# Gradient of a gated block with a long convolution, one core: dh for two slabs per matmul, dw stored by ScalarE's queue

## The chip, the core and the metric

The kernel runs as one program on one core of a Trainium2 chip. The metric is the device time of an execution in microseconds (us); every kernel is run several times. Nothing but this kernel runs on the core during a measurement.

The core's engines are named as the profile names them: PE (TensorE, matmuls), PEld (the weight loads of those matmuls), DVE (VectorE), ACT (ScalarE), POOL (GpSimd) and SP (SyncE). Each runs its own instructions in order. SP, ACT and POOL also issue transfers (DMAs); the profile writes "SPq", "ACTq" and "POOLq" for that.

## The reference

What is computed is the forward result of one block and its gradients for nine inputs. The block takes x of 2048 rows and 1024 columns, and weights of 1024 by 3584 (gate, up) and 3584 by 1024 (down):

```python
x = A_q
xn = _layernorm(x, axis=-1)
s = _A_ref(xn, A_k, A_v, A_shift_k, A_ssm_k, A_ssm_D)   # shift by 4 taps, long convolution, times xn
g = _silu(_B_ref(xn, B_w_gate, B_w_up, B_w_down))
return x + s * g

def _B_ref(x, w_gate, w_up, w_down):
    g = jnp.einsum("bsd,df->bsf", x, w_gate)
    u = jnp.einsum("bsd,df->bsf", x, w_up)
    h = g * u
    return jnp.einsum("bsf,fd->bsd", h, w_down)
```

and the outputs are `_out` with the nine results of `jax.vjp(_f, ...)(grad_out)`. The part that matters here is the gradient of the gated product: dh = dbm @ w_down transposed (dbm is the gradient of the block's B result), then dg = dh * u and du = dh * g, then the weight gradients dw_gate = xn transposed @ dg, dw_up = xn transposed @ du, and dw_down = h transposed @ dbm.

## The kernel before

The hidden width of 3584 is cut into 14 slabs (`NSL`) of 256 columns (`SLW`). The kernel runs in stages that overlap:

1. 0 to about 515 us: layer norm, the gate and up products slab by slab (`gu_unit`, L671), and beside them on DVE the forward convolution (`conv_forward`). The products g and u of each slab go to DRAM (`GUd`), as do h and its transpose.
2. To about 700 us: the down product (`bm_mm`, L1034) and, row block by row block, the gate's derivative on DVE (`gate`). dbm goes to DRAM and comes back transposed (`DBMT`, four tiles of 512 rows).
3. 700 to about 1317 us, the stage of the change: `dh_half` (L1471 to L1493) and `dw_slab` (L1495 to L1512).
4. To about 1498 us: dw_down (`dwd_mm`, L1582). Then dx (`dx_part`, L1644) with the layer norm's backward, to the end at 1909.9 us. Beside it DVE computes the gradients of the shift (`dk_units`).

Stage 3 in detail. For a slab and one half of the rows (1024), `dh_half` makes dh in two groups `g` of four row blocks. One PSUM tile `psb` (128 by 512 values) holds two row blocks `x` of 256 columns: 16 matmuls of 256 columns (L1482), whose moving operand is `wdt`, w_down of this slab transposed by the load (`load_wdt`, L1330). ACT copies the tile to `dht` (L1484). `multiply` then multiplies, on DVE, g and u of that half slab (`dgu`, loaded from `GUd` by `gu_in`) by dh, in place, for four row blocks at a time; after the second group the product is stored to `DGd`, from which stage 4 loads it again.

`dw_slab` makes dw_gate and dw_up of a slab together: for each of eight `dc` it adds 16 matmuls of 512 columns (L1499: 256 of gate, 256 of up) over the 16 row blocks. The first 8 read the first half slab, the last 8 the second half. ACT copies the tile to `wb` (L1504), and after each second `dc` two transfers of 128 KB on SP's queue store it (L1508).

The two are interleaved: after each `dc` group, `next(others, None)` lets the generator of the next slab's dh run one group `g`, so that the four dh groups of the next slab lie behind `dc` 0 to 3, and `dc` 4 to 7 follow with no dh between them. `todo` holds the multiplies; `after_group` puts them on DVE after the next group of matmuls, and then calls `btick`, which advances `conv_backward` on DVE by as much as `BT` says (2 ticks for a dw group, 1 for a dh tile). From L1530 on, DVE's instructions keep this program order (`PIN`). `conv_backward` (L1103) begins with the eight transforms of `dy_forward`, each of which ends with a store `DYFd<-DX` on POOL's queue (L1101), and goes on with 16 units of `product` (whose first tile is `m`, L342) and `inv8`.

The loads of `GUd` for later half slabs are issued on SP after each `dw_slab` (L1546), one `wdt` load after `dc` 3 (L1511). The five tiles U11, U6, U2, U3 and U12 take the half slabs in turn.

`Wbc` (L128, loaded at L152) holds the four taps of the shift for all 1024 channels on every partition. `shift` (L762) and `dk_units` (L1230) read it.

SP's, POOL's and ACT's transfers use a common set of eight completion semaphores per kind (hardware queues of SP and ACT; POOL's own), taken in turn: a transfer waits, on its issuing engine, until the earlier one of the same semaphore has landed.

Of the kernel before, what the change touches and what calls it, by code (L numbers as in the profile page):

```python
# [19 lines left out]
def build_kernel(  # L20
# [11 lines left out]
    nc = tc.nc  # L32
# [92 lines left out]
    nc.scalar.activation(warm[:], warm[:], ACT.Sqrt)  # L125
    RSTD = const.tile([P, NB], F32, name="RSTD")
    RSTN = const.tile([P, NB], F32, name="RSTN")
    Wbc = const.tile([P, 4, D], BF16, name="Wbc")  # L128

    tip = tc.alloc_tile_pool(name="tip", bufs=1)  # L130
    TI = tip.tile([P, 2, 8, 2, P], BF16, name="TI")
# [9 lines left out]
    def load_bcast(bsb):  # L141

        wrow = bsb.tile([1, D, 4], BF16, name="wrow")
        st(wrow[:].rearrange("p d j -> p (d j)"), A_shift_k.rearrange("(o d) j -> o (d j)", o=1))
        wtap = bsb.tile([1, 4, D], BF16, name="wtap")

        def turn(j):
            nc.gpsimd.tensor_copy(wtap[:, j, :], wrow[:, :, j])

        def spread():  # L150
            st(WTd.rearrange("(o x) -> o x", o=1), wtap[:].rearrange("p j d -> p (j d)"))
            st(Wbc[:].rearrange("p j d -> p (j d)"), bass.AP(WTd.tensor, WTd.offset, [[0, P], [1, 4 * D]]))  # L152
        return turn, spread

    def angles(tg):
# [378 lines left out]
    Dz = kst.tile([P, D], BF16, name="Dz")  # L534
    V.memset(Dz[:], 0.0)
    krow = kst.tile([P, 2, 11, 256], BF16, name="k")
    V.memset(krow[0:1, 0, 0:3, :], 0.0)
    bsb = pool("bc_sb", 1)
    tg = pool("tg", 1)
# [200 lines left out]
    def conv_forward():  # L740
        S_ = conv_state

        def load_kv(dp, c):
            S_["k", dp] = krow
            if dp > 0 or c == 0:
                for i in range(2) if dp == 0 else (c,):
                    cld_k(krow[:, i], i, dp)
            if dp > 0 or c == 1:
                for i in range(2) if dp == 0 else (c,):
                    v = U[4][:, 2048 * i:2048 * i + 2048].rearrange("p (a x) -> p a x", a=8)  # L750
                    cld_v(v, i, dp * 256, 256)
# [6 lines left out]
        def shift(dp):  # L758
            kv = cx.tile([P, NB, 256], BF16, name="kv")
            S_["kvt", dp] = kv  # L760
            k = S_.pop(("k", dp))
            wb = lambda j: Wbc[:, j:j + 1, dp * 256:(dp + 1) * 256].unsqueeze(1).to_broadcast([P, 2, 8, 256])  # L762
# [12 lines left out]
            yield 2.3  # L775
# [294 lines left out]
    while conv_state["filters"]:  # L1070
        bm_first([fc_])
        fc_ += 1
    bw = pool("bw", 2, side="right")
    mh = [pool("mh0", 1, side="right")]
    ps_bx = pool("ps_bx", 1, space=PSUM)

# [106 lines left out]

    def dh_tail(ds, G, ew):
        hr = ew.tile([P, 2, 8, P], BF16, name="yl")
        ho = ew.tile([P, 2, P, 8], BF16, name="ho")
# [12 lines left out]
        st(o_dssmk[ds * P:(ds + 1) * P, :], ho[:].rearrange("p c u r -> p (c u r)"))  # L1199
        yield 0.0  # L1200
# [3 lines left out]
    def dk_units(ew):  # L1204
# [9 lines left out]
        def load_turned(i):  # L1214
# [7 lines left out]
                nc.sync.dma_start_transpose(out=dkT[:], in_=DKSHd[ds, c * H:c * H + H, :])  # L1222
            return kT, dkT

        dk = load_rows(0)
        yield 3
        for i in range(16):
            ds, c = divmod(i, 2)
            dsl = slice(ds * P, (ds + 1) * P)
            wb = lambda j: Wbc[:, j:j + 1, dsl].to_broadcast([P, 8, P])  # L1230
# [95 lines left out]
            defer(turn)  # L1326

    def load_wdt(sl):
        wdt = bw.tile([P, DC, SLW], BF16, name="wdt")
        wdt_ld[0] = nc.sync.dma_start_transpose(out=wdt[:], in_=B_w_down[sl * SLW:(sl + 1) * SLW, :])  # L1330
        return wdt

    def load_ht(bp):
        ht = mh[bp % 2].tile([P, NF, 256], BF16, name="ht")
# [1 line left out]
            last = ld(ht[:, f0:f1], ht_rows(bp, f0, f1))  # L1336
        return (lambda fc: ht[:, fc]), last

    DGU = {}
    wdts = []  # L1340
    wdt_ld = [None]

    def gu_in(k):

        if k < 2 * NSL:
            t = U[(11, 6, 2, 3, 12)[k % 5]][:].rearrange("p (a b f) -> p a b f", b=8, a=2)
            ld(t, GUd[k // 2, k % 2])
            DGU[k] = t

    with tc.issue_after(ht1[1].ins):  # L1350
        ht2 = load_ht(2)
    bm_first(range(fc_, NF))
    room = [bw.tile([P, DC, SLW], BF16, name="wdt")[:].rearrange("p (i x) f -> p i (x f)", i=2) for i in range(2)]
# [61 lines left out]
    for bp in range(2, 8):  # L1415
# [6 lines left out]
        with tc.issue_after(row_ld[0].ins):  # L1422
            if bp in (4, 5, 7):
                q = (4, 5, 7).index(bp)
                dma_t = nc.sync.dma_start_transpose(out=DBMT[q], in_=DBMd[512 * q:512 * q + 512, :])
            if bp == 6:
                wdts.append(load_wdt(0))
                dma_t = wdt_ld[0]
        with tc.issue_after(dma_t.ins) if dma_t is not None else nullcontext():
            rows_in[2 * bp + 1] = gate_rows(2 * bp + 1)  # L1430
        if bp > 5:
            with tc.issue_after(row_ld[0].ins):
                gu_in(0) if bp == 6 else wdts.append(load_wdt(1))
        for i in range(2):
            n = (2 * bp + i - 2) * NF
            while done < n + NF:
# [11 lines left out]

    XN = [u8(q, a=4) for q in (7, 0, 1, 9)]
    bg = pool("bg", 2, side="right")  # L1450
    U.append(bg.tile([P, 4096], BF16, name="U12", bufs=1))
    ps_b = ps_tr = pool("ps_b", 4, space=PSUM)
    tr_name[0] = "psb"
    ps_c3 = pool("ps_c3", 2, space=PSUM)
# [6 lines left out]
        bpump((bcnt[0] - 10) / (BT - 10))  # L1461

    todo = []

    def after_group(n):
        flush(2)
# [1 line left out]
            todo.pop(0)()  # L1468
        btick(n)

    def dh_half(k, wdt):  # L1471

        sl, hf = divmod(k, 2)
        dgu = DGU[k]
        for g in range(2):
            dht = bg.tile([P, 4, SLW], BF16, name="dht", bufs=3)
            for e in range(2):
                ps = ps_b.tile([P, 512], F32, name="psb")
                for x in range(2):
                    b = 4 * g + 2 * e + x  # L1480
                    for dc in range(DC):
                        nc.tensor.matmul(ps[:, x * SLW:(x + 1) * SLW], DBMT[2 * hf + g][:, dc, (b % 4) * P:(b % 4 + 1) * P],  # L1482
                                         wdt[:, dc, :], start=(dc == 0), stop=(dc == DC - 1))
                nc.scalar.copy(out=dht[:, 2 * e:2 * e + 2].rearrange("p b f -> p (b f)"), in_=ps[:])  # L1484
                after_group(1)

            def multiply(g=g, dht=dht):
                bs = slice(4 * g, 4 * g + 4)
                tt(dgu[:, :, bs], dgu[:, :, bs], dht[:].unsqueeze(1).to_broadcast([P, 2, 4, SLW]), MUL)
                if g == 1:  # L1490
                    ld(DGd[sl, :, 1024 * hf:1024 * hf + 1024, :].rearrange("a (u b) f -> u a b f", u=P), dgu)
            todo.append(multiply)
            yield  # L1493

    def dw_slab(sl, dgus, others):  # L1495
        for dc in range(DC):
# [21 lines left out]

    for e in later:
        e[0] = -2  # L1520
    for k in (1, 2):
        gu_in(k)
    for q in range(4):
        ld(XN[q], xnn[:, q // 2, 4 * (q % 2):4 * (q % 2) + 4, :])
    for k in (3, 4):
        gu_in(k)
    DBM = [u8(q, a=4) for q in (10, 8, 4, 5)]
    HSL = (3, 11, 6)
    hs = {}
    PIN[0] = PINQ[0] = True  # L1530
    for k in range(2):
        run(dh_half(k, wdts[0]))
    todo.pop()()
    for sl in range(NSL):
        if sl + 1 == NSL:
            load_h(0)
            for q in range(4):
                ld(DBM[q], DBMd[512 * q:512 * q + 512, :].rearrange("(b u) d -> u b d", u=P))
            load_h(1)

        def halves():
            for k in (2 * sl + 2, 2 * sl + 3):
                if k < 2 * NSL:
                    yield from dh_half(k, wdts[sl + 1])
        dw_slab(sl, [DGU[2 * sl], DGU[2 * sl + 1]], halves())
        for k in (2 * sl + 5, 2 * sl + 6):  # L1546
            gu_in(k)
# [260 lines left out]
```

## Time and profile before

| | |
|---|---|
| runs | 1911.66 us median of 3 (1911.64 to 1913.55) |
| the profiled execution | 1911.63 us, of which 1909.9 us are the span of its instructions |
| granted clock of TensorE | 1.0 of full speed |
| PE, DVE, ACT, POOL busy | 1899.4, 1549.7, 636.8, 332.7 us |
| bytes moved | 444.34 MB, mean 233 GB/s |
| stage 3 | 700 to 1317 us |

How to read it: the span is the time from the first to the last instruction that the profile shows; what lies around it is 1911.63 - 1909.9 = 1.7 us. A group line gives the source line, the engine, the operation, output and input tiles, shapes, the count, then busy time and mean ns of one, then the engine's idle time just before these instructions and what ended it. Matmuls overlap, so the mean of one (its own length with its pipeline) is longer than the distance from one to the next; the distance is read from a timeline, whose rows give start, length, engine, line and count of a run of equal instructions.

### The profile page before, as it was taken

What the parts mean: (1) busy time and instruction counts of PE and PEld (TensorE: products, weight loads), DVE (VectorE), ACT (ScalarE), POOL (GpSimd) and SP (SyncE); (2) the same over time, 40 slices, a digit from 0 to 9 for tenths busy, and PEclk for the clock granted to TensorE, in tenths of its full rate; (3) what the DMA queues carried; (4) which work ended last, traced back from release to release, by engine and by line L of the source; (5) the groups of instructions that cost most, each with busy time, mean ns of one, the idle gap of its engine ahead of it and who ended that gap; (6) DMA issues with size and microseconds to landing.
All of it is one profiled execution on the core that took longest, in us unless ns stands there. A gap on an engine that the chain in (4) does not pass through costs nothing.

```text
span 1909.9 us, 28150 instructions
## 1 busy us (share of the span) xinstructions
PE 1899.4 (99%) x11379; PEld 1013.9 (53%) x11379; DVE 1549.7 (81%) x1711; ACT 636.8 (33%) x927; POOL 332.7 (17%) x465
## 2 busy tenths in 40 slices
PE   8999999999999999999999999999999999999999
PEld 5555555545444466666666665664444444444444
DVE  8999999999988556887999999999995305788862
ACT  5765555556333233432222222222222102111121
POOL 5121211201113220001031221211212101111120
PEclk9999999999999999999999999999999999999999
DMA  9777766769769997677897798585887999989852
GB/s 298 269 263 233 251 208 223 252 211 311 241 227 307 316 314 231 209 231 233 264 277 247 231 266 258 184 286 180 230 238 181 219 206 190 194 187 190 194 166 88
DMA packets 425106, 444.34 MB, mean 233 GB/s; under 512 B 268400, under 2 KB 342796, under 8 KB 410512
## 3 DMA queue, kind: packets, MB, share of 16 engines
q1 hardware_dynamic: 367504, 239.03, 45.9%
q0 software_dynamic: 41152, 174.15, 29.0%
q10 hardware_dynamic: 16320, 29.36, 4.1%
q8 instruction: 89, 1.46, 0.3%
q14 instruction: 41, 0.34, 0.1%
HBM read 193.87 MB, written 189.84 MB: 201 GB/s over the span
## 4 chain that ended last, share of the span: by engine, by line
PE 97%; DVE 1%; ACT 1%; DMA 0%; issue 0%; SPq 0%; ACTq 0%
PE psb L1499 20%; PE psx L1644 20%; PE psg L671 19%; PE psb L1482 10%; PE psbm L1034 10%; PE psb L1582 9%; PE psF L234 3%; PE psI L455 1%; PE tr L565 1%; PE psY L1193 1%; PE psY L445 1%; PE psx L1582 1%; DVE bst L578 0%; DMA wslab<-in_B_w_gate_dram 0%; PE tr L788 0%; DVE U L212 0%
## 5 line engine op out<-in xcount | busy, mean ns | idle before, releaser
L671 PE MATMUL psg<-wslab,U 128*128 128x512 bf16 x1792 | 401.8, 379 | 3.5 <-DMA wslab<-in_B_w_gate_dram 2.1
L1499 PE MATMUL psb<-U,U 128*128 128x512 bf16 x1792 | 397.1, 379 | 0.0
L1644 PE MATMUL psx<-U,dgut 128*128 128x512 bf16 x1536 | 332.8, 379 | 0.0
L1644 PEld LDWEIGHTS <-dgut 128*128 128x128 bf16 x1792 | 175.3, 98 | 211.4
L1499 PEld LDWEIGHTS <-U 128*128 128x128 bf16 x1792 | 175.2, 98 | 198.0
L671 PEld LDWEIGHTS <-U 128*128 128x128 bf16 x1792 | 172.6, 98 | 197.2 <-issue 3.6
L1482 PE MATMUL psb<-wdt,U 128*128 128x256 bf16 x1792 | 205.6, 273 | 0.0
L1482 PEld LDWEIGHTS <-U 128*128 128x128 bf16 x1792 | 175.2, 98 | 29.2
L212 DVE TENSOR_TENSOR W<-W 128x1024 f32<-128x1024 f32 (+1 forms) x189 | 186.5, 1003 | 4.1
L1582 PE MATMUL psb<-U,U 128*128 128x512 bf16 x816 | 177.3, 379 | 0.0
L1504 ACT CAST wb<-psb 128x512 bf16<-128x512 f32 x112 | 65.6, 586 | 315.4 <-PE psb L1499 310.5
L1249 DVE SCALAR_TENSOR_TENSOR dkp<-dkT,kT 128x1024 bf16<-128x1024 bf16 (+2 forms) x64 | 78.3, 1223 | 93.1 <-DMA dkT<-DKSHd 91.4
L1034 PE MATMUL psbm<-U,ht 128*128 128x512 bf16 x672 | 146.0, 379 | 0.0
L1582 PEld LDWEIGHTS <-U 128*128 128x128 bf16 x896 | 87.4, 98 | 104.4
L673 ACT CAST gut<-psg 128x512 bf16<-128x512 f32 x156 | 91.5, 589 | 120.2 <-PE psg L671 119.7
L1676 ACT ACTIVATE dx_t<-dxn 128x1024 bf16<-128x1024 f32 x15 | 15.9, 1057 | 324.7 <-DVE dxn L212 324.7
L1034 PEld LDWEIGHTS <-ht 128*128 128x128 bf16 x672 | 65.7, 98 | 78.1
L212 DVE TENSOR_TENSOR U<-U,dht 128x2048 bf16<-128x2048 bf16 x56 | 68.3, 1220 | 46.5 <-ACT dht L1484 46.5
L1484 ACT CAST dht<-psb 128x512 bf16<-128x512 f32 x112 | 65.6, 587 | 116.4 <-PE psb L1482 116.4
L66 POOL DMA_DIRECT2D Hd<-hN x54 | 36.6, 677 | 268.9 <-DVE hN L212 258.9
L1623 ACT CAST wbs<-psb 128x512 bf16<-128x512 f32 x51 | 29.9, 586 | 145.4 <-PE psb L1582 134.3
L212 DVE TENSOR_TENSOR W<-SP 128x1024 f32<-128x1024 f32 x64 | 74.1, 1218 | 1.3 <-ACT SP L295 0.8
(263 smaller groups left out, 2342.9 us busy)
## 6 DMA issues: line engine op xcount, KB each, us to landing
U<-GUd SPq DMA_DIRECT2D x28, 1024.0 KB, 9.3
DGd<-U SPq DMA_DIRECT2D x28, 1024.0 KB, 5.8
GUd<-gut ACTq DMA_DIRECT2D x39, 512.0 KB, 5.2
out_dram<-wb SPq DMA_DIRECT2D x112, 128.0 KB, 4.8
U<-Hd SPq DMA_DIRECT2D x14, 1024.0 KB, 6.6
Hd<-hN POOLq DMA_DIRECT2D x54, 256.0 KB, 4.5
HTd<-hT SPq DMA_DIRECT2D x24, 512.0 KB, 3.7
ht<-HTd SPq DMA_DIRECT2D x18, 512.0 KB, 7.5
```

Of the source, the lines that this page charges most:

```text
L212: pinned(V.tensor_tensor(o, a, b, op))
L234: mm = nc.tensor.matmul(ps[:, k].rearrange("p (c d) -> p c d", c=2), T[:, r, k, :], xr[:, r], start=(n == 0), stop=(n == len(rs) - 1 and ( ...
L671: gu_mm[0] = nc.tensor.matmul(ps[:], XNT[q][:, dc, qi * P:(qi + 1) * P], w[:, dc].rearrange("p a f -> p (a f)"), start=(dc == 0), stop=(dc ...
L673: nc.scalar.copy(out=gut[:, :, i], in_=ps[:].rearrange("p (a f) -> p a f", a=2))
L1034: mm = nc.tensor.matmul(ps[:, dh * 512:(dh + 1) * 512], ht(fc)[:, i * P:(i + 1) * P], WD[fc // 4][:, fc % 4, dh * 512:(dh + 1) * 512], sta ...
L1249: ins = V.scalar_tensor_tensor(prod[:].rearrange("p r d -> p (r d)")[:, lo:H], dkT[:, 0, lo:H], 1.0, kT[:, 0, 13 + m + lo:13 + m + H], op0 ...
L1482: nc.tensor.matmul(ps[:, x * SLW:(x + 1) * SLW], DBMT[2 * hf + g][:, dc, (b % 4) * P:(b % 4 + 1) * P], wdt[:, dc, :], start=(dc == 0), sto ...
L1484: nc.scalar.copy(out=dht[:, 2 * e:2 * e + 2].rearrange("p b f -> p (b f)"), in_=ps[:])
L1499: nc.tensor.matmul(ps[:], XN[b // 4][:, b % 4, dc * P:(dc + 1) * P], dgus[b // 8][:, :, b % 8], start=(b == 0), stop=(b == NB - 1))
L1504: nc.scalar.copy(out=wb[:, dc % 2].rearrange("p a f -> p (a f)"), in_=ps[:])
L1582: nc.tensor.matmul(ps, h[:, f, b, :], DBM[b // 4][:, b % 4, dh * 512:(dh + 1) * 512], start=(b == 0), stop=(b == NB - 1))
L1644: nc.tensor.matmul(ps[:, dh * 512:(dh + 1) * 512], t[n][:, f, i * P:(i + 1) * P], WGU[n][:, f, dh * 512:(dh + 1) * 512], start=(n == 0 and ...
```

## The change

- `dh_half` becomes `dh_pair(p, hf)`: slabs 2p and 2p+1 together. A PSUM tile holds one row block `x` and both slabs: 8 matmuls of 512 columns, whose moving operand takes 256 columns of each of two `wdt` halves. `dht` holds both slabs; group 0 uses a tile of the pool, group 1 the unused half of the table tile `TI` (`dht_own`). A multiply handles both slabs, two instructions instead of one.
- Both halves of pair 0 (where both halves of the first slab alone were made before) come ahead of the first `dw_slab`. Then, during an even slab, the first half of the next pair's rows is made behind `dc` 4 to 7, and during an odd slab the second half behind `dc` 2 to 5.
- `wdt` is kept for pairs, in two places. The loads of the pair after next are called in an even slab at `dc` 1 and `dc` 5.
- Six tiles (U11, U6, U12, U2, U13, U3) for half slabs, taken in the order in which they come free. After an even slab the second halves of the next pair are loaded, after an odd slab the first halves of the pair after it.
- The dw stores go from SP's queue to ACT's (`sta`).
- To make room, `Wbc` is gone: two pieces of 256 channels (`WB`) for the shift, loaded as they are needed, the first 512 channels on SP's queue and the others on POOL's; and `wbk`, 256 channels at a time, two buffers, in `dk_units`, on POOL's queue. `ho` shares the room of `vl`.

In the built program the two `wdt` loads of every pair stand directly behind each other on SP's queue, with no other transfer between them.

```diff
-    Wbc = const.tile([P, 4, D], BF16, name="Wbc")
...
-            st(Wbc[:].rearrange("p j d -> p (j d)"), bass.AP(WTd.tensor, WTd.offset, [[0, P], [1, 4 * D]]))
+            load_taps(WB[:].rearrange("p j e d -> p j (e d)"), 0, 512, ld)
...
+    WB = kst.tile([P, 4, 2, 256], BF16, name="WB")
+
+    def load_taps(t, d0, w, queue=st):
+        queue(t, bass.AP(WTd.tensor, WTd.offset + d0, [[0, P], [D, 4], [1, w]]))
...
+            if dp > 1 and c == 0:
+                load_taps(WB[:, :, dp % 2], dp * 256, 256)
...
+            if i % 4 == 0:
+                wbk = ew.tile([P, 4, 256], BF16, name="wbk", bufs=2)
+                load_taps(wbk[:], ds * P, 256)
...
     def load_wdt(sl):
-        wdt = bw.tile([P, DC, SLW], BF16, name="wdt")
-        wdt_ld[0] = nc.sync.dma_start_transpose(out=wdt[:], in_=B_w_down[sl * SLW:(sl + 1) * SLW, :])
-        return wdt
+        wdt_ld[0] = nc.sync.dma_start_transpose(out=WDT[sl // 2 % 2][:, sl % 2], in_=B_w_down[sl * SLW:(sl + 1) * SLW, :])
...
-    def dh_half(k, wdt):
-
-        sl, hf = divmod(k, 2)
-        dgu = DGU[k]
+    def dh_pair(p, hf):
+
+        if 2 * p >= NSL:
+            return
+        both = (2 * p, 2 * p + 1)
         for g in range(2):
-            dht = bg.tile([P, 4, SLW], BF16, name="dht", bufs=3)
-            for e in range(2):
+            dht = bg.tile([P, 4, 2, SLW], BF16, name="dht", bufs=1)[:] if g == 0 else dht_own
+            for x in range(4):
                 ps = ps_b.tile([P, 512], F32, name="psb")
-                for x in range(2):
-                    b = 4 * g + 2 * e + x
-                    for dc in range(DC):
-                        nc.tensor.matmul(ps[:, x * SLW:(x + 1) * SLW], DBMT[2 * hf + g][:, dc, (b % 4) * P:(b % 4 + 1) * P],
-                                         wdt[:, dc, :], start=(dc == 0), stop=(dc == DC - 1))
-                nc.scalar.copy(out=dht[:, 2 * e:2 * e + 2].rearrange("p b f -> p (b f)"), in_=ps[:])
+                for dc in range(DC):
+                    nc.tensor.matmul(ps[:].rearrange("p (j f) -> p j f", j=2), DBMT[2 * hf + g][:, dc, x * P:(x + 1) * P],
+                                     WDT[p % 2][:, :, dc, :], start=(dc == 0), stop=(dc == DC - 1))
+                nc.scalar.copy(out=dht[:, x].rearrange("p j f -> p (j f)"), in_=ps[:])
                 after_group(1)
+                if x == 1:
+                    yield
 
             def multiply(g=g, dht=dht):
                 bs = slice(4 * g, 4 * g + 4)
-                tt(dgu[:, :, bs], dgu[:, :, bs], dht[:].unsqueeze(1).to_broadcast([P, 2, 4, SLW]), MUL)
-                if g == 1:
-                    ld(DGd[sl, :, 1024 * hf:1024 * hf + 1024, :].rearrange("a (u b) f -> u a b f", u=P), dgu)
+                for j, sl in enumerate(both):
+                    dgu = DGU[sl, hf]
+                    tt(dgu[:, :, bs], dgu[:, :, bs], dht[:, :, j].unsqueeze(1).to_broadcast([P, 2, 4, SLW]), MUL)
+                    if g == 1:
+                        ld(DGd[sl, :, 1024 * hf:1024 * hf + 1024, :].rearrange("a (u b) f -> u a b f", u=P), dgu)
             todo.append(multiply)
             yield
...
-                    ld(dst[rows, fs].rearrange("(c p) f -> p c f", p=P), wb[:, :, a])
+                    sta(dst[rows, fs].rearrange("(c p) f -> p c f", p=P), wb[:, :, a])
             after_group(2)
-            if dc == 3 and sl + 2 < NSL:
-                wdts.append(load_wdt(sl + 2))
-            next(others, None)
+            if 0 <= dc - (2 if sl % 2 else 4) < 4:
+                next(others, None)
+            if sl % 2 == 0 and dc in (1, 5) and sl + 4 < NSL:
+                load_wdt(sl + 4 + dc // 5)
...
+    for hf in range(2):
+        run(dh_pair(0, hf))
     todo.pop()()
     for sl in range(NSL):
...
-        dw_slab(sl, [DGU[2 * sl], DGU[2 * sl + 1]], halves())
-        for k in (2 * sl + 5, 2 * sl + 6):
-            gu_in(k)
+        dw_slab(sl, [DGU[sl, 0], DGU[sl, 1]], dh_pair(sl // 2 + 1, sl % 2))
+        gu_room += [DGU_U[sl, 0], DGU_U[sl, 1]]
+        for k in ((sl + 2, 1), (sl + 3, 1)) if sl % 2 == 0 else ((sl + 3, 0), (sl + 4, 0)):
+            gu_in(*k)
```

More of the change, by code (lines that the diff above doesn't have):

```diff
@@ L761, in shift @@
             k = S_.pop(("k", dp))
-            wb = lambda j: Wbc[:, j:j + 1, dp * 256:(dp + 1) * 256].unsqueeze(1).to_broadcast([P, 2, 8, 256])
+            wb = lambda j: WB[:, j:j + 1, dp % 2].unsqueeze(1).to_broadcast([P, 2, 8, 256])
             room = cx.tile([P, 16, 256], BF16, name="KX")[:].rearrange("p a x -> p (a x)") if dp == 0 else U[7][:]
@@ L1072, in build_kernel @@
         fc_ += 1
-    bw = pool("bw", 2, side="right")
+    bw = pool("bw", 1, side="right")
+    WDT = [bw.tile([P, 2, DC, SLW], BF16, name="wdt0")]
     mh = [pool("mh0", 1, side="right")]
@@ L1185, in dh_tail @@
         hr = ew.tile([P, 2, 8, P], BF16, name="yl")
-        ho = ew.tile([P, 2, P, 8], BF16, name="ho")
+        ho = ew.tile([P, 2, P, 8], BF16, name="ho", tag="vl")
         for c in range(2):
@@ L1223, in load_turned @@
             return kT, dkT
+        wbk = None
         dk = load_rows(0)
@@ L1229, in dk_units @@
             dsl = slice(ds * P, (ds + 1) * P)
-            wb = lambda j: Wbc[:, j:j + 1, dsl].to_broadcast([P, 8, P])
+            if i % 4 == 0:
+                wbk = ew.tile([P, 4, 256], BF16, name="wbk", bufs=2)
+                load_taps(wbk[:], ds * P, 256)
+            wb = lambda j: wbk[:, j:j + 1, ds % 2 * P:(ds % 2 + 1) * P].to_broadcast([P, 8, P])
             acc = ew.tile([P, 8, P], BF16, name="dka")
@@ L1337, in load_ht, with gu_in @@
         return (lambda fc: ht[:, fc]), last
-    DGU = {}
-    wdts = []
+    DGU, DGU_U = {}, {}
     wdt_ld = [None]
[L1343 to L1348, printed above, removed]
+    gu_room = [11, 6, 12, 2, 13, 3]
+    def gu_in(sl, hf):
+        if sl < NSL:
+            DGU_U[sl, hf] = gu_room.pop(0)
+            DGU[sl, hf] = U[DGU_U[sl, hf]][:].rearrange("p (a b f) -> p a b f", b=8, a=2)
+            ld(DGU[sl, hf], GUd[sl, hf])
     with tc.issue_after(ht1[1].ins):
@@ L1352, in build_kernel @@
     bm_first(range(fc_, NF))
-    room = [bw.tile([P, DC, SLW], BF16, name="wdt")[:].rearrange("p (i x) f -> p i (x f)", i=2) for i in range(2)]
+    room = [WDT[0][:, n].rearrange("p (i x) f -> p i (x f)", i=2) for n in range(2)]
     bms = [out_of(pss[i], room[0][:, i]) for i in range(2)]
@@ L1426, in build_kernel @@
             if bp == 6:
-                wdts.append(load_wdt(0))
+                load_wdt(0)
                 dma_t = wdt_ld[0]
@@ L1432, in build_kernel @@
             with tc.issue_after(row_ld[0].ins):
-                gu_in(0) if bp == 6 else wdts.append(load_wdt(1))
+                gu_in(0, 0) if bp == 6 else load_wdt(1)
         for i in range(2):
@@ L1450, in build_kernel @@
     bg = pool("bg", 2, side="right")
-    U.append(bg.tile([P, 4096], BF16, name="U12", bufs=1))
+    U += [bg.tile([P, 4096], BF16, name=f"U{i}", bufs=1) for i in (12, 13)]
+    WDT.append(bg.tile([P, 2, DC, SLW], BF16, name="wdt1", bufs=1))
     ps_b = ps_tr = pool("ps_b", 4, space=PSUM)
@@ L1463, in build_kernel @@
     todo = []
+    dht_own = TI[:, 1].rearrange("p r k f -> p (r k f)").rearrange("p (x j f) -> p x j f", x=4, j=2)
     def after_group(n):
@@ L1520, in build_kernel @@
         e[0] = -2
-    for k in (1, 2):
-        gu_in(k)
+    for k in ((1, 0), (0, 1), (1, 1)):
+        gu_in(*k)
+    for sl in (2, 3):
+        load_wdt(sl)
     for q in range(4):
         ld(XN[q], xnn[:, q // 2, 4 * (q % 2):4 * (q % 2) + 4, :])
-    for k in (3, 4):
-        gu_in(k)
+    for k in ((2, 0), (3, 0)):
+        gu_in(*k)
     DBM = [u8(q, a=4) for q in (10, 8, 4, 5)]
@@ L1530, in build_kernel @@
     PIN[0] = PINQ[0] = True
-    for k in range(2):
-        run(dh_half(k, wdts[0]))
+    for hf in range(2):
+        run(dh_pair(0, hf))
     todo.pop()()
     for sl in range(NSL):
-        if sl + 1 == NSL:
+        if sl + 2 == NSL:
             load_h(0)
@@ L1538, in build_kernel @@
                 ld(DBM[q], DBMd[512 * q:512 * q + 512, :].rearrange("(b u) d -> u b d", u=P))
+        if sl + 1 == NSL:
             load_h(1)
[L1541 to L1544, printed above, removed]
-        dw_slab(sl, [DGU[2 * sl], DGU[2 * sl + 1]], halves())
-        for k in (2 * sl + 5, 2 * sl + 6):
-            gu_in(k)
+        dw_slab(sl, [DGU[sl, 0], DGU[sl, 1]], dh_pair(sl // 2 + 1, sl % 2))
+        gu_room += [DGU_U[sl, 0], DGU_U[sl, 1]]
+        for k in ((sl + 2, 1), (sl + 3, 1)) if sl % 2 == 0 else ((sl + 3, 0), (sl + 4, 0)):
+            gu_in(*k)
         if 0 < sl < 5:
```

## The prediction, as put on record before the run

> **What bounds the kernel now.** I read the busy times first, then the chain of waits, then the groups, and last the timelines of the stretch that the change touches.
>
> The busy times and, from further down on the page, the shares of the chain of waits and the groups on the change's own path:
>
> ```profile
> PE 1899.4 (99%) x11379; PEld 1013.9 (53%) x11379; DVE 1549.7 (81%) x1711; ACT 636.8 (33%) x927; POOL 332.7 (17%) x465
> ...
> PE 97%; DVE 1%; ACT 1%; DMA 0%; issue 0%; SPq 0%; ACTq 0%
> ...
> L1499 PE MATMUL psb<-U,U 128*128 128x512 bf16 x1792 | 397.1, 379 | 0.0
> ...
> L1482 PE MATMUL psb<-wdt,U 128*128 128x256 bf16 x1792 | 205.6, 273 | 0.0
> ...
> L1504 ACT CAST wb<-psb 128x512 bf16<-128x512 f32 x112 | 65.6, 586 | 315.4 <-PE psb L1499 310.5
> ...
> L212 DVE TENSOR_TENSOR U<-U,dht 128x2048 bf16<-128x2048 bf16 x56 | 68.3, 1220 | 46.5 <-ACT dht L1484 46.5
> ```
>
> PE is the bound: 1899.4 of 1909.9 us, and dh and dw wait for nothing in front of them (0.0 at both ends of those rows). ACT and DVE wait for PE. So the change can gain only where PE's own work shrinks, and can lose only where PE is made to wait.
>
> The timeline of PE around one change of slab (start, length, line, count):
>
> ```profile
> 905.99 3.66 PE L1482 MATMUL psb<-wdt,U 128*128 128x256 bf16 x32
> 909.49 3.62 PE L1499 MATMUL psb<-U,U 128*128 128x512 bf16 x16
> 912.94 3.66 PE L1482 MATMUL psb<-wdt,U 128*128 128x256 bf16 x32
> 916.43 3.62 PE L1499 MATMUL psb<-U,U 128*128 128x512 bf16 x16
> 919.88 3.66 PE L1482 MATMUL psb<-wdt,U 128*128 128x256 bf16 x32
> 923.38 17.43 PE L1499 MATMUL psb<-U,U 128*128 128x512 bf16 x80
> ```
>
> From start to start, 32 matmuls of 256 columns take 909.49 - 905.99 = 3.50 us, then 3.49 and 3.50 (mean 3.497, 109 ns each). 16 of 512 columns take 3.45 us twice; the run of 80 takes until the next start at 940.64, so 17.26 us, 215.8 ns each. PE works per column; a narrow matmul costs hardly more than half a wide one. The mean lengths 379 and 273 ns overlap and would mislead.
>
> **The change part by part.**
>
> *dh with 512 columns.* 1792 matmuls of 256 become 896 of 512, 56 sets of 32 become 56 of 16. Each set saves 3.497 - 3.452 = 0.045 us: 56 x 0.045 = 2.5 us. The rounding of the starts (0.035 to 0.05) gives 2.0 to 2.8. The strided moving operand, 256 columns of each of two halves, has no row of its own; I price it as L1499. Its bounds are 215.8 ns and two narrow ones, 218.6 ns, at which the gain is nothing. I take the first, since stride shows nowhere as a price in these rows. Evictions stay 112 of 0.586 us and multiplies 56 of 1.22 us.
>
> By the Trainium skill, page "TensorE: Matmul & The Clock Gate", section "Back-to-back issue gap", sustained matmuls of 512 columns can run at about 131 ns; dh would then be 896 x 131 = 117 us. The 80 matmuls above, at 215.8 ns with a granted clock of 1.0, disagree, so I give this no weight in the sum.
>
> *dw stores on ACT's queue.* 112 issues. ACT's own stores of this size of work (GUd) take 0.521 us of issue, SP's dw stores have a median of 0.454: 112 x 0.52 = 58 us more on ACT, which waits 315.4 us in front of these very casts and 116.4 us in front of dh's. Behind each issue waits the next cast. Casts follow each other at 1.73 us at the closest (dht, 921.83 to 923.58), and cast, issue and another cast need 0.59 + 0.52 + 0.59 = 1.70; PE also has four `psb` tiles in hand. Cost 0. Without that cover it would be up to 58 us. The bad case is an issue that itself waits for something on SP's queue: a rival below.
>
> *Two halves of pair 0 ahead of the first dw slab.* The sets of its second slab (two halves, 4 sets of 16) stand 13.8 us earlier and are missing later; the sum is the same. One small gain: around 731 to 744 the trace has some 0.76 us of PE gaps where dh alternates with the small psF matmuls; 0 to 0.76 of it may go. I take 0.
>
> *Tables in pieces (WB, wbk).* SP issues 0.5 MB behind the table's store near 27.5 us, and needs nothing else until its next store at 63. POOL issues 2 + 4 loads at 0.55 to 0.85 us each, 5 us in all, on an engine busy 17%. DVE, which uses them, is 81% busy and PE is not waiting there. Cost 0, bounds 0 to 1 us (one load of DYFd's landing beyond its median, 9.9 - 5.3, mostly covered).
>
> *w_down loads.* The same 14 of them, but the two of a pair stand directly behind each other on SP's queue: 2 x 4.9 us of issue by the median, 2 x 12.8 at worst (the row of L1330: 1700/4910/12837 ns, landing at most 21.7 us later). Behind them queue the `U<-GUd` loads, of median landing 9.3 us. The pair is used more than a slab later, and the gu loads have about 28 us before their multiply: 25.7 issue at worst leaves a little; by the median there is plenty. Cost 0.
>
> *The hand-over of dh to dw.* This is the one new deadline. Before, the last multiply of a slab's half followed dh by four or more dw groups; now, in odd slabs, dh stands behind dc 2 to 5 and only two dw groups (dc 6, 7) follow. The slab after begins with tiles that are multiplied early; the one that is late is needed 12 matmuls in. From the end of the last dht cast to that need: 2 x 3.45 + 12 x 0.216 - 0.79 (cast and its wait) = 8.7 us, less the multiply's 1.22, so DVE may be 7.5 us late; with four groups it could be 14.4. The timeline of DVE shows the place where it is late:
>
> ```profile
> 894.78 1.29 DVE L283 SCALAR_TENSOR_TENSOR DX<-W,W 128x512 bf16<-128x512 f32 x2
> 896.00 1.28 DVE L283 SCALAR_TENSOR_TENSOR DX<-W 128x512 bf16<-128x512 f32 x2
> 907.56 4.56 DVE L212 TENSOR_TENSOR m<-TF,B 128x4096 bf16<-128x4096 bf16 x3 [10.28 <-issue]
> 912.04 1.22 DVE L212 TENSOR_TENSOR U<-U,dht 128x2048 bf16<-128x2048 bf16 x1
> ...
> 934.72 1.22 DVE L212 TENSOR_TENSOR U<-U,dht 128x2048 bf16<-128x2048 bf16 x1
> ```
>
> DVE waits 10.28 us because `m` may overwrite only when the last DYFd store of DX has landed; this multiply stands behind `m` on DVE. How long the store takes is in the view of the DMA issues of 897.3 to 898.0 (KB each, median us to landing):
>
> ```profile
> DYFd<-DX POOLq DMA_DIRECT2D x1, 1024.0 KB, 9.9
> ```
>
> The same store lands in 4.8 to 9.9 us, median 5.3, over its 8 issues. In the changed order the multiply of the next slab (U13) stands again right behind the three `m`. DX ends at about 899.6 there (897.28 and two multiplies of 1.22 that now come before). The multiply is done at 899.6 + 0.3 + L + 4.48 + 1.2 = 905.6 + L, where L is the landing. The need: that slab starts 13.8 us after 895.6, less the 1.0 saved by then, 908.4, plus 12 matmuls, 911.0. PE waits L - 5.4, at least nothing. With L = 5.3 that is 0, with 9.9 it is 4.5 us. In the new order no transpose and no gu load stands just ahead on SP; beside the store lie two dw stores and one read of A_q. So I take L near 6, stall 0.5 us; ends 0 and 4.5. The other five hand-overs of odd slabs have no such store in front: 0.
>
> By the Trainium skill, page "DMA: Bandwidth & Descriptors", section "Queues, rings and completion order", the DMA engines take the queues' rows in turn. A third queue, ACT's, would then lengthen POOL's store: my estimate of half as long again, 5.3 x 1.5 = 8.0, gives a stall of 2.6 us and no net change in time. No row of the profile shows three queues at once here.
>
> **Sum.** -2.5 + 0.5 = -2.0 us. Span 1909.9 - 2.0 = 1907.9; with the 1.7 us around it 1909.6. The profiled execution, 1911.63, lies at the median of the runs, 1911.66, so no correction.
>
> **The rivals.** What can be told from no change is 0.2%, 3.8 us: below 1907.8 is faster, above 1915.5 slower.
>
> *Slower: DVE hands U13 over late.* Mechanism: L above; place: the start of the slab at about 908 us; it decides the sign from L = 5.4 + 2.5 = 7.9 on, and 0.2% from L = 11.7 on. For it: the three POOL loads issued right behind the store (vl, B, kshl) landed in 15.2 to 18.1 us, so the queues are full there; at L = 15 to 18 PE waits 9.6 to 12.6 us, time 1919 to 1922. Against it: the store itself landed in 9.9 at most, and that was beside two gu loads.
>
> *Slower: ACT stuck behind SP.* If a dw store on ACT must wait until an SP transfer that shares its completion count has landed (gu loads up to 21.8 us), the casts behind it are late, and PE runs out of `psb` tiles after about 18 us (four tiles at 3.45 and the queue in front): 21.8 - 18 = 3.7 us each, at most 7 changes of slab, 26 us. Against it: 39 GUd stores sit on ACT's queue now at 520 to 522 ns, without any wait. Time up to 1911.7 - 2.5 + 26 = 1935, more likely 1913 to 1918.
>
> *The change does not do what it says.* The two w_down loads are not four groups apart in the order; if the 512-column form is paced as two of 256 the gain is nothing: 1911.7.
>
> *Faster by over 0.2%.* 2.8 from pacing and 0.76 of gaps make 3.6 us, 1908.1; it needs 0.2 us more, from the start, where `wslab` waits 2.1 us for its DMA. Nothing in the trace says that goes.
>
> **How the numbers follow.** Forecast (1907.8 to 1911.7, likeliest 1909.6): 0.52. No gain, or a stall that eats it (to 1915.5): 0.20, still within 0.2%. Late hand-over beyond 3.8 us: 0.10. ACT behind SP: 0.05. Faster than 1907.8: 0.13, the skill's pace 0.01 of it. So faster 0.13, same 0.72, slower 0.15. The range 1907.6 to 1915 leaves out about 0.1 below and 0.1 above or a little more.
>
> **What would show it.** dh at 3.45 us a set of 16 (right) or 3.50 (no gain). On PE, a gap in front of L1499 near 911 us (late hand-over), beside the landing of the last DYFd store. ACT's dw store issues at 0.52 us, or with a tail of many us. L1330's issues and the gu loads behind them: a gap at other changes of slab would make my "cost 0" wrong. A shift of the whole PE work before 700 us would be something that I have not priced.

## The result, and the profile after

| kernel | median us (lowest to highest, runs) | ratio to before, 95% interval |
|---|---|---|
| before | 1912.32 (1911.64 to 1913.55, 6) | |
| changed | 1918.00 (1916.55 to 1923.76, 6) | 1.0033 [1.0020, 1.0046] |

The change makes the kernel 5.7 us slower; the forecast was 2.0 us faster, within a range that ended at 1915.0. The profiled execution is the slowest of the six: 1923.76 us, span 1922.0.

The busy times, the chain of waits and the groups of the changed kernel (dht's second tile is now called TI, so the multiplies and the casts appear under two names):

```profile
PE 1901.0 (99%) x10483; PEld 927.3 (48%) x10483; DVE 1548.7 (81%) x1711; ACT 636.8 (33%) x927; POOL 341.7 (18%) x470
...
PE 89%; DMA 3%; DVE 3%; SPq 3%; ACT 1%; issue 0%; POOL 0%; ACTq 0%; DVEq 0%; POOLq 0%
...
L1513 PE MATMUL psb<-U,U 128*128 128x512 bf16 x1792 | 397.5, 379 | 0.0
...
L1492 PE MATMUL psb<-wdt,U 128*128 128x512 bf16 x896 | 203.5, 381 | 2.6 <-ACT wb L1518 2.6
...
L1518 ACT CAST wb<-psb 128x512 bf16<-128x512 f32 x112 | 65.5, 587 | 324.4 <-PE psb L1513 274.1
```

PE's share of the chain fell from 97% to 89%. dh (L1492), which waited for nothing before, now waits 2.6 us for ScalarE's cast of dw; and that cast's idle time, of which the dw matmuls ended 310.5 of 315.4 us before, is now ended by other things for 50 of 324.4 us: 22.1 by w_down loads, 19.0 by the dw stores' own landing, the rest by a `DGd` store and by dh. Where PE waits for it, its timeline around 1012 to 1029 us shows:

```profile
1012.66 1.91 PE L444 MATMUL psY<-B,TI 128*128 128x256 bf16 x16
1014.41 1.89 PE L1492 MATMUL psb<-wdt,U 128*128 128x512 bf16 x8
1018.89 3.35 PE L1492 MATMUL psb<-wdt,U 128*128 128x512 bf16 x8 [2.59 <-ACT wb L1518]
1022.04 3.88 PE L1513 MATMUL psb<-U,U 128*128 128x512 bf16 x16
1025.76 3.62 PE L1492 MATMUL psb<-wdt,U 128*128 128x512 bf16 x16
1029.21 1.03 PE L1513 MATMUL psb<-U,U 128*128 128x512 bf16 x4
```

ScalarE's timeline, SP's, the landing of the first load, and the chain of waits (start, length, what) in the same stretch:

```profile
1002.50 0.59 ACT L1518 CAST wb<-psb 128x512 bf16<-128x512 f32 x1 [2.87 <-PE psb L1513]
1010.43 7.71 ACTq L72 DMA_DIRECT2D out_dram<-wb  x2
1018.26 1.07 ACT L1518 CAST wb<-psb 128x512 bf16<-128x512 f32 x2 [15.17 <-DMA wdt<-in_B_w_down_dram]
```

```profile
988.68 22.50 SPq L1339 DMA_TRANSPOSE wdt<-in_B_w_down_dram  x2
1011.29 3.13 SPq L61 DMA_DIRECT2D DGd<-U  x2
```

```profile
wdt<-in_B_w_down_dram SPq DMA_TRANSPOSE x1, 21.7
```

```profile
990.99 26.75 DMA wdt<-in_B_w_down_dram
```

Read them from the bottom. The second w_down load lands at 990.99 + 26.75 = 1017.74. ScalarE's last cast ended at 1003.09, and its dw store should follow at once, since its data are there. Its two transfers are issued at 1010.43 and, at the end of that run of 7.71 us, at 1017.76, right behind the second load's landing. (The first load, issued at 988.68, landed 21.7 us later by the view of the DMA issues: 1010.4, the moment of the first transfer. SP's queue, too, moves on only at 1011.29.) Only then does ScalarE cast again, and PE, which had filled its `psb` tiles, had stood for 2.59 us.

In the built program every transfer that SP or ScalarE issues gets one of eight completion counters in turn and first waits until the transfer before it on that counter has landed; POOL's have counters of their own. The order around that pair of loads:

```
SP   wdt<-in_B_w_down   counter 5
SP   wdt<-in_B_w_down   counter 6
SP   DGd<-U x2          counters 7, 0
ACT  out_dram<-wb x2    counters 1, 2
SP   U<-GUd x2          counters 3, 4
ACT  out_dram<-wb x2    counters 5, 6   waits for both loads
```

All five pairs of loads within the dw stage have a pair of dw stores in that place. In this execution two of them make ScalarE wait for a load: this one, and one for 6.96 us at 923.7, behind which PE shows no gap.

The gap costs more than its length. The windows before and over it (length, busy time of PE, PEld, DVE, ACT and POOL, then the granted clock, DMA share, GB/s):

```profile
1000.00:1014.40 14.40, 14.40 (x76) 7.27 (x75) 14.16 (x14) 0.59 (x1) 0.00 (x0) 1.00 1.08 170
1014.40:1022.40 8.00, 5.41 (x19) 2.05 (x18) 0.62 (x1) 1.07 (x2) 0.00 (x0) 0.80 1.10 373
```

From the third matmul behind the gap to 1022.5 us they start 0.43 us apart instead of 0.216. Together the place costs 4.4 us. The rest of what this execution lost lies in the stage behind dw: transposes of w_gate took up to 31.52 us to issue (at most 9.41 before), and PE lost about 9 us between 1451 and 1483, in gaps and at the lower clock behind them. The next experiment tells which of the two belongs to the change.

### The profile page after: what moved, and what is told of

It reads as the page before. It is cut to its first block, busy times and chain, and to the rows that moved or that the text cites. A ratio compares the mean times of both kernels' runs of the same rounds, so it can differ in the third digit from the quotient of the medians.

```text
span 1922.0 us, 26253 instructions
## 1 busy us (share of the span) xinstructions
PE 1901.0 (99%) x10483; PEld 927.3 (48%) x10483; DVE 1548.7 (81%) x1711; ACT 636.8 (33%) x927; POOL 341.7 (18%) x470
## 4 chain that ended last, share of the span: by engine, by line
PE 89%; DMA 3%; DVE 3%; SPq 3%; ACT 1%; issue 0%; POOL 0%; ACTq 0%; DVEq 0%; POOLq 0%
PE psx L1658 20%; PE psb L1513 19%; PE psg L674 18%; PE psbm L1039 10%; PE psb L1492 10%; PE psb L1596 4%; PE psF L233 3%; SPq L1582 2%; DMA wdt<-in_B_w_down_dram 1%; PE psI L454 1%; DMA B<-KFd 1%; PE tr L568 1%; PE psx L1596 1%; PE psY L444 1%; DMA U<-in_A_q_dram 1%; DVE W L211 1%
## 5 line engine op out<-in xcount | busy, mean ns | idle before, releaser
L1513 PEld LDWEIGHTS <-U 128*128 128x128 bf16 x1792 | 175.4, 98 | 208.2 <-issue 0.8
L674 PEld LDWEIGHTS <-U 128*128 128x128 bf16 x1792 | 172.6, 98 | 197.4 <-issue 3.3
L1492 PE MATMUL psb<-wdt,U 128*128 128x512 bf16 x896 | 203.5, 381 | 2.6 <-ACT wb L1518 2.6
L1518 ACT CAST wb<-psb 128x512 bf16<-128x512 f32 x112 | 65.5, 587 | 324.4 <-PE psb L1513 274.1
L1596 PEld LDWEIGHTS <-U 128*128 128x128 bf16 x896 | 87.5, 98 | 107.9 <-DMA U<-Hd 3.6
L1492 PEld LDWEIGHTS <-U 128*128 128x128 bf16 x896 | 87.9, 98 | 106.2 <-issue 4.2
L233 PEld LDWEIGHTS <-TF 128*128 128x128 bf16 x560 | 53.9, 98 | 18.3 <-issue 2.9
L211 DVE TENSOR_TENSOR HX<-W 128x1024 bf16<-128x1024 f32 (+3 forms) x66 | 62.1, 990 | 0.1
## 6 DMA issues: line engine op xcount, KB each, us to landing
U<-GUd SPq DMA_DIRECT2D x28, 1024.0 KB, 10.8
```

The lines of the kernel that those rows point to most:

```text
L211: pinned(V.tensor_tensor(o, a, b, op))
L233: mm = nc.tensor.matmul(ps[:, k].rearrange("p (c d) -> p c d", c=2), T[:, r, k, :], xr[:, r], start=(n == 0), stop=(n == len(rs) - 1 and ( ...
L674: gu_mm[0] = nc.tensor.matmul(ps[:], XNT[q][:, dc, qi * P:(qi + 1) * P], w[:, dc].rearrange("p a f -> p (a f)"), start=(dc == 0), stop=(dc ...
L1492: nc.tensor.matmul(ps[:].rearrange("p (j f) -> p j f", j=2), DBMT[2 * hf + g][:, dc, x * P:(x + 1) * P], WDT[p % 2][:, :, dc, :], start=(d ...
L1513: nc.tensor.matmul(ps[:], XN[b // 4][:, b % 4, dc * P:(dc + 1) * P], dgus[b // 8][:, :, b % 8], start=(b == 0), stop=(b == NB - 1))
L1518: nc.scalar.copy(out=wb[:, dc % 2].rearrange("p a f -> p (a f)"), in_=ps[:])
```

## The experiments

Theory A: ScalarE stands still in dw stores that count behind w_down loads. Theory B: with three queues all transfers are slower. Theory C came after the first runs: two loads side by side delay everything, and the counter is a bystander. All runs of the kernel before that were timed beside these had medians of 1911.82 to 1912.13.

**again: the changed kernel once more.**

> The changed kernel once more, for a second trace. Theory A (a dw store on ScalarE's queue waits for the two w_down loads, because they count on the same completion counters): the PE gap of about 2.7 us in front of dh, with the half-speed matmuls behind it (4.4 us together), is there again behind a pair of w_down loads that lands in over 20 us, near 1016 or at another pair. Theory B (the transfers are slower everywhere, with three queues at work): the gaps of 1450 to 1480 us (9 us together) are there again as well. If they are gone, they belong to that one execution. Time 1917 to 1919 in either case.

1917.74 us (1915.37 to 1919.63), ratio 1.0030 [1.0019, 1.0042]. ScalarE's and PE's timeline of this execution:

```profile
1012.35 9.93 ACTq L72 DMA_DIRECT2D out_dram<-wb  x2
1022.40 1.07 ACT L1518 CAST wb<-psb 128x512 bf16<-128x512 f32 x2 [17.25 <-DMA wdt<-in_B_w_down_dram]
```

```profile
1023.04 3.57 PE L1492 MATMUL psb<-wdt,U 128*128 128x512 bf16 x8 [4.68 <-ACT wb L1518]
```

The gap came back at the same place, 7.0 us with the slow matmuls behind it, and a smaller one of 2.1 us at 764, where ScalarE waited 6.59 us for an earlier w_down load. The gaps of 1451 to 1482 are gone: they belonged to that one execution, and why its transposes were slow there stays open. The sum nearly holds: 7.0 + 2.1 - 2.2 (the gain, below) = 6.9, of the 8.0 between this execution (1919.63) and the profiled one before (1911.63). The idle times also give PE's cover at this place, what ScalarE may stand idle before PE stands: 15.17 - 2.59 = 12.6 us and 17.25 - 4.68 = 12.6 us. It is no constant. The same difference is 9.1 and 10.9 us at the two gaps of dw_on_sp below, 10.8 in share_sp and 9.1 in ring7; and at 764 a wait of 6.59 us already cost 2.1, since there PE waited for another work of ScalarE, its copies of `psF` (L294).

**dw_on_sp: the dw stores back on SP's queue.**

```diff
-                    sta(dst[rows, fs].rearrange("(c p) f -> p c f", p=P), wb[:, :, a])
+                    ld(dst[rows, fs].rearrange("(c p) f -> p c f", p=P), wb[:, :, a])
```

> The changed kernel with the dw stores back on SP's queue, all else as changed. Theory A: ScalarE has no store left that waits for a w_down load; its casts wait for the stores' landing only, the gap of 4.4 us near 1016 goes: 1910 to 1914. Theory B (crowding): the stores are the same bytes, so 1915 to 1919. A late hand-over of dh to dw would show as a gap in front of the dw matmuls at the start of an even slab, in both kernels alike.

1931.06 us, 1.0103 [1.0087, 1.0118]: far outside what either theory said. SP's and ScalarE's timeline:

```profile
902.04 19.71 SPq L1339 DMA_TRANSPOSE wdt<-in_B_w_down_dram  x2
```

```profile
938.16 0.58 ACT L1518 CAST wb<-psb 128x512 bf16<-128x512 f32 x1 [14.82 <-DMA out_dram<-wb]
```

Behind the two loads the stores now stand in the queue itself; they land late, the three `wb` tiles run out, and PE waits 5.9 us at 933 and 8.0 us at 1028, by the distances of the starts. So with the pair of loads in this place both queues lose, and the stores' move to ScalarE's queue is not what makes the loss: the loss is smaller with the move than without.

**b_sta: the kernel before, with only the stores moved to ScalarE.** The edit is the same line, the other way.

> The kernel before with only the dw stores moved to ScalarE's queue. Theory A: the stores wait for SP's transfers here too, but the w_down loads come singly and land sooner; ScalarE shows waits of a few us, PE little: 1912 to 1914. Theory B: more queues alone make it slower: 1915 or more. If the store move were free as predicted: 1911.5 to 1912.5.

1911.87 us, 1.0001 [0.9992, 1.0009]. The move alone costs nothing and brings nothing, as the prediction had it; the loads there come singly. The few us of waits that theory A expected on ScalarE do not show: PE ended all 313.6 us of the idle time in front of these casts.

**apart and apart_b: the two loads held apart.**

```diff
-                    sta(dst[rows, fs].rearrange("(c p) f -> p c f", p=P), wb[:, :, a])
+                    if sl % 2 == 0 and dc == 3 and sl + 4 < NSL:
+                        tc.keep_in_program_order(ld(dst[rows, fs].rearrange("(c p) f -> p c f", p=P), wb[:, :, a]))
+                    else:
+                        sta(dst[rows, fs].rearrange("(c p) f -> p c f", p=P), wb[:, :, a])
...
                 load_wdt(sl + 4 + dc // 5)
+                tc.keep_in_program_order(wdt_ld[0])
```

> The changed kernel with one pair of dw stores of each even slab (dc 3) put on SP's queue between the two w_down loads, held in that order: so the loads are some groups apart in time, 108 of the 112 stores less a few stay on ScalarE. Theory A: each load lands in 5 to 15 us rather than 14 to 27, ScalarE's waits for them get short, no PE gap near 1016: 1910 to 1914. Theory B: 1915 to 1919. If the gu loads behind the held second load come late, a gap in front of dw at another slab shows it.

> The kernel with the loads held apart once more, since one of its eleven runs took 1916.3 us: 1909.7 to 1910.5 in most, no PE gap of over 1 us between 700 and 1500 us.

1910.25 us (0.9996 [0.9987, 1.0004]) and 1911.13 us (0.9992 [0.9984, 1.0001]). No gap of PE in the dw stage, and the first time is in the range of theory A; the second missed its own expectation, with four of its eleven runs at 1910.5 or below. And the reason given was not the right one: a load still lands in a median of 13.4 and 11.2 us (14.0 and 12.3 in the two executions of the changed kernel), hardly in less. Besides, the pins had also moved both loads behind the gu loads on SP's queue. pin_only, next, and pin_sp, further down, tell these apart.

**pin_only: pinned, but side by side.** The second part of the edit above alone.

> The changed kernel with the w_down loads held in program order among the pinned instructions: they come later on SP's queue, behind the gu loads, but still directly behind each other, and at four of five pairs one dw store on ScalarE still counts on a counter of theirs, some eight transfers later. Theory A: what matters is when that store comes after the load; later than in the changed kernel, so shorter waits: 1910 to 1914. Theory C: side by side is enough to lose: 1915 to 1919.

> The kernel with the loads pinned once more: 1910 to 1911, which with the eleven runs there are tells it from the kernel before (1.6 us, 0.09%).

1910.35 us (0.9992 [0.9983, 1.0000]), and in the second run (pin_b) 1911.64 us (0.9998 [0.9989, 1.0006]), 0.6 above its expectation. SP's and ScalarE's timeline of the first:

```profile
996.04 20.56 SPq L1339 DMA_TRANSPOSE wdt<-in_B_w_down_dram  x2
```

```profile
1003.17 0.90 ACTq L72 DMA_DIRECT2D out_dram<-wb  x2
```

Two loads side by side, with 20.6 us of issue, harm nothing here: the stores at 1003 and 1010 go out at once, since the transfers eight places earlier were others. Theory C falls: two loads side by side are not enough to lose.

**share_sp: only the stores that count behind the loads moved to SP.** `ld` instead of `sta` for five pairs of stores; PE, DVE and POOL run the same order as in the changed kernel.

> The changed kernel, in which only the five pairs of dw stores that count on the same counters as the two w_down loads (dc 5 of slab 0, dc 1 of slabs 2, 4, 6, 8) are issued by SP's queue; the two loads stay directly behind each other, and PE, DVE and POOL run the same order. Theory A (ScalarE's queue stands still in a store that waits for the count): no idle time of ScalarE for w_down loads, the gap near 1016 goes, 1909.5 to 1912. Theory C (two loads side by side delay all transfers, the count is a bystander): ScalarE waits for the landing of dw stores, a gap of 3 us or more stays, 1915 to 1919.

1919.08 us, 1.0030 [1.0021, 1.0040]. The numbers of theory A were wrong; the time is at the upper end of what theory C gave, and ScalarE did wait for the landing of dw stores too (15.7 us in three places). The gap has another cause. ScalarE:

```profile
1028.04 0.59 ACT L1518 CAST wb<-psb 128x512 bf16<-128x512 f32 x1 [17.31 <-DMA DGd<-U]
```

It stands still all the same, 17.3 us, now for a DGd store: the next dw store counts behind that, and the DGd store stands behind the loads on SP's queue. Taking one link out of the ring puts the next one in its place. PE stands 6.47 us behind it. The theory has to be put wider: ScalarE waits for SP's queue through the counters, and the early pair of loads makes that queue late.

**ring7 and ring7_pool: the counter alone.** Pinned loads as in pin_only (1910.35), and behind each pair seven loads of 128 bytes, on SP's queue or on POOL's:

```diff
+                if dc == 5:
+                    for i in range(7):
+                        tc.keep_in_program_order(nc.sync.dma_start(out=DUM[0:1, 64 * i:64 * i + 64], in_=B_w_gate[0:1, 0:64]))
```

> The kernel with the loads pinned (side by side, behind the gu loads) plus seven loads of 128 bytes each on SP's queue behind every pair of w_down loads; their data are not used. They take seven of the eight completion counters, so the dw stores that ScalarE issues next count on the second w_down load or on a tiny load that stands behind it, as in the changed kernel. Theory A: ScalarE stands still for 10 us or more at several pairs, PE gaps where this exceeds some 14 us, 1912 to 1920. Theory C, or the loads' place on the queue alone: seven tiny loads cost nothing, 1910 to 1911.5.

> The control: the same seven tiny loads on GpSimd's queue, which has counters of its own; PE, DVE and ScalarE run the same order as with them on SP's queue. Both theories: 1910 to 1911.5, no idle time of ScalarE for w_down loads.

On SP: 1920.01 us (1912.28 to 1931.51), 1.0043 [1.0022, 1.0065]. On POOL: 1910.68 us, 0.9996 [0.9988, 1.0005]. The engines' order is the same in both but for the tiny loads. ScalarE and PE with them on SP:

```profile
750.43 16.08 ACTq L72 DMA_DIRECT2D out_dram<-wb  x2
766.55 0.59 ACT L1520 CAST wb<-psb 128x512 bf16<-128x512 f32 x1 [18.27 <-DMA dum<-in_B_w_gate_dram]
```

```profile
767.18 6.05 PE L1494 MATMUL psb<-wdt,U 128*128 128x512 bf16 x16 [9.17 <-ACT wb L1520]
```

ScalarE waits 18.27 us for a load of 128 bytes whose data nobody uses, only because its store counts behind it and it stands behind the w_down loads. That is the mechanism by itself. In this execution (1928.34 us) ScalarE waited so at three places, for 28.2 + 4.7 us in all; the times of the eleven runs lie 19 us apart. With the tiny loads on POOL's queue no cast of dw waits for a load. What stays open: no run left the pair in its early place and freed all of ScalarE's stores from counting behind SP's transfers. That this alone would bring the time back is concluded from the traces, not tested.

**pin_sp: pinned loads, all dw stores on SP.**

> The kernel with the loads pinned, and the dw stores on SP's queue. Theory A: stores behind 10 to 20 us of w_down issue are late, the three wb tiles run out, ScalarE's cast waits for their landing, PE gaps of 3 us or more: 1914 to 1930. If the place of the loads alone mattered: 1910 to 1912, and the move of the stores to ScalarE was not needed.

1911.45 us, 1.0000 [0.9992, 1.0009]: a miss for what theory A said of it, and within what the other case gave. In that order four dw store transfers fall between the two loads of a pair and hold them apart. With the loads pinned, it makes no difference that these runs can tell which queue stores dw.

**apart_256: the gain of the wide matmuls alone.** The kernel of apart, with dh as two runs of 8 matmuls of 256 columns into the halves of a tile.

> The kernel with the loads held apart, but dh with 256 columns again (two runs of 8 matmuls into the halves of a tile, 1792 matmuls): the gain of the wide matmuls alone, 2.15 us by the starts in the traces (2.5 by the prediction): 1912 to 1913 beside 1910.2 of the wide form. If the gain of that kernel comes from elsewhere: within 0.5 us of the wide form.

1913.31 us against 1911.13 of apart_b, timed beside it: 2.18 us for the wide form, and 2.24 between their lowest runs (1912.22 and 1909.98). Summed from start to start, the dh matmuls take 195.63 us in the trace of apart_256 and 193.39 in that of apart_b: 2.24 us, a little more than the 2.15 of the expectation. That the medians agree so closely is luck: the runs lie 9 and 4 us apart, and drawing anew from the runs of each puts the difference of the medians anywhere from 0.9 to 3.6 us.

## Why the prediction was wrong

**dh with 512 columns: right.** 2.5 us forecast, bounds 2.0 to 2.8. PE's starts give 3.45 us for 16 in the timeline above (1025.76 to 1029.21), 3.497 was the set of 32, and summed over all sets the starts give 2.24 us; the runs gave 2.18. The strided operand costs nothing that the starts show. The pace of about 131 ns from the Trainium skill's page "TensorE: Matmul & The Clock Gate", section "Back-to-back issue gap", shows in no run here.

**dw stores on ACT's queue, "Cost 0", and w_down loads, "Cost 0": these steps failed, together.** In place of 0 the two cost some 7.9 us (5.7 us slower in spite of 2.2 gained). Each was priced by its own engine's free time: ScalarE had the room for 112 issues (right: b_sta; that its casts at 921.83 and 923.58 are 1.75 us apart and not 1.73 changes nothing), and the loads were due more than a slab later (right: no dh waited for `wdt`). What was not priced is what the two do to each other: a store that ScalarE issues waits for a load on SP's queue that nothing in its data needs. The rival "ACT stuck behind SP" had the mechanism and, with 1913 to 1918, the time, but a chance of only 0.05, and gu loads as its cause where the w_down loads were it. The argument against it, that the GUd stores go out at 0.52 us without a wait, came from a stage in which no pair of loads of 20 us stood on SP's queue. Its sizes were off as well: 18 us of cover where 9.1 to 12.6 were there, no slow clock behind the gap, and so 3.7 us for each of seven stalls, where one of 4.4 and, in the second trace, two of 7.0 and 2.1 came. The sign that it named, dw store issues with a long tail, is not in the row of these issues (0.38 us by the median, 2.3 at most): the wait stands in front of the issue, in the idle time of the next cast.

**The two loads were called four dw groups apart, and stood side by side.** The text saw this and priced it as issue time of SP. The calls at `dc` 1 and `dc` 5 place nothing: the room for both comes free at the same moment, behind the last dh of the slab before (988.5 us), and the order on SP puts both there, ahead of DGd stores and gu loads. Before, the load came singly.

**The hand-over of dh to dw: right, 0 of the 0.5 us.** The last DYFd store landed in 5.5 us (near 6 was taken, 8.0 estimated for three queues at work), and PE shows no gap there. DVE and PE of the changed kernel:

```profile
908.30 2.35 DVE L211 TENSOR_TENSOR U<-U,TI 128x2048 bf16<-128x2048 bf16 x2
```

```profile
902.12 24.34 PE L1513 MATMUL psb<-U,U 128*128 128x512 bf16 x112
```

The first of the two multiplies is that of U13; it ended at 908.30 + 1.22 = 909.5, against a forecast of 905.6 + 5.5 = 911.1. DX ended at 897.9, 0.6 us later than before and not at 899.6: the two multiplies ahead of it did not delay it by their whole length. The new slab starts 32 matmuls into PE's row, at 909.0, and needs U13 12 matmuls later, at 911.6 (forecast 911.0). So the slack was 2.1 us and not next to nothing: the result is right, its terms are 1.6 and 0.6 us off.

**The net of -2.0 us is, at best, that of the kernels without the stall,** and a part of it comes and goes: four series of them (apart, apart_b, pin_only, pin_b) have medians of 1910.25 to 1911.64, which is 0.2 to 1.8 us below the kernel before as timed beside them, and lowest runs of 1909.8 to 1910.0, 1.2 to 1.6 us below its lowest. PE and DVE in pin_b, an execution of 1912.91:

```profile
1587.59 1.22 DVE L1259 SCALAR_TENSOR_TENSOR dkp<-dkT,kT 128x1024 bf16<-128x1024 bf16 x1 [74.55 <-DMA dkT<-DKSHd]
```

```profile
1605.02 7.28 PE L1659 MATMUL psx<-U,dgut 128*128 128x512 bf16 x33 [2.04 <-DVE dxn L211]
```

DVE's last wait for dkT ended between 1579.4 and 1587.6 in the kernels without the stall; in the two traces with a PE gap behind it (apart and pin_b) it ended at 1586.2 and 1587.6, but apart_256 had 1586.3 and no gap. PE comes there 1.8 to 2.0 us earlier than before and can find DVE late. That this is why the gain is sometimes lost was not tested. None of these kernels is shown to be faster than before beyond its interval; pin_only is the nearest.

## What to carry to other kernels

A free engine is not a free queue: when stores are moved to another engine's queue, look up what each of them waits for in the built program, completion counters included, and how late the transfer eight places earlier can be. A call in the source does not set the time of a load; the moment at which its room comes free does, so two loads into room that is freed together were issued together here. When an engine behind the bound can stall, its price is the stall less the cover (near 1016 us 15.2 to 17.3 less 12.6 us) and what the slower clock adds (1.7 to 2.2 us). The cover is read from the buffers in hand at that place, not from the engine's mean idle time; here it was 9.1 to 12.6 us from place to place, and less where PE waits for other work of the stalled engine.

## What was not expected of the hardware

A gap of 2.59 us is enough for the granted clock to fall to 0.80 over the 8 us around it (0.50 from 1019.2 to 1022.5), and the matmuls behind it cost 1.7 us more; after 4.68 us it was 2.2 us. By the Trainium skill, page "TensorE: Matmul & The Clock Gate", section "HAM oscillation — how this bites in real kernels", the rule is to have no gap of more than some 3.4 us; here a shorter one was enough. The length alone does not decide: in ring7 two waits of 1.87 and 0.32 us at 862 were followed by a clock of 0.57 over 864 to 868, while in pin_b 2.04 us at 1603 left it at 1.00.

The w_down loads of the kernel before landed in 9.3 us by the median; the two of the pair near 990 us, beside POOL's loads of the next product, took 21.7 and 26.7 us. Why it is that much was not tried.
